# Fused Nystrom attention and SiLU layer: the first q and k loads on another queue, and the order of some early and later matmuls

## The chip, the cores and the metric

The kernel runs on one core of one Trainium2 chip. The metric is the device time of one execution in microseconds (us), lower is better. Every time below is in us unless it says ns.

## What is computed

```python
# q, k, v: (8 batches, 8 heads, 576 tokens, 64)
q_lm, k_lm = mean of q, k over groups of 18 tokens      # 32 landmarks
A  = softmax(scale * q    @ k_lm.T)                       # 576 x 32
Bm = softmax(scale * q_lm @ k_lm.T)                       # 32 x 32
C  = softmax(scale * q_lm @ k.T)                          # 32 x 576
Z  = Bm.T / (norm1(Bm) * norminf(Bm) + 1e-06)
for _ in range(6): Z = 2 * Z - Z @ Bm @ Z
x  = concat over heads of (A @ Z @ C @ v)                 # (4608, 512)
h  = x @ w_in                                             # (4608, 2048)
out = (h * sigmoid(h)) @ w_out                            # (4608, 512)
```

All inputs and the output are float32; the matmuls take bfloat16.

## The kernel before

**Order of work.** The kernel fixes the order of each engine's instructions by hand: an instruction stands on its engine where the Python code emits it. The loop has eight periods, one for each batch `b`. In period `b` the two big layers of batch `b` run (`l1_mm` makes `hps`, `l1_act` puts Silu of it into `gT`, `l2_mm` makes `ops`, which ScalarE copies to `ost` and SyncE stores), while the attention of batch `b + 1` (class `Att`) is worked out in between. A period has 16 steps `s`; `d` (2, 3, then 0) is the step at which the attention stages begin. `x @ w_in` is never formed directly: `m_unit` and `m_pair` make `mb`, a product of `zwT` with columns of `w_in`, and `l1_mm` multiplies it with `AT`, the transposed A.

**Counts.** After each step's `l1_mm` and `act`, `l2_mm(n)` emits up to `n` second-layer matmuls of 128x512 from a queue of finished token tiles; 16 of them make an output tile. How many each step emits stands in the lists `CNT` (periods 0 and 1) and `REST` (all others). These matmuls wait for nothing new, so they are what fills TensorE between dependent stages. In steps where ScalarE changes between Exp and Silu it loads a table (L151).

**The opening (L114 to L145, L759 to L845).** For batch 0 there is no earlier work to overlap. `load_qk(0)` issues four loads on POOL's DMA queue, in the order `j` = 1, 0, 3, 2: k and q of heads 0 to 3, then k and q of heads 4 to 7. Each is 128 rows (32 landmarks of four heads) of 18 tokens x 64, float32 in HBM and bfloat16 in the tile `nat`; the cast is done by the DMA. Behind them on POOL come `affine_select`, the load of v, the four quarters of w_in and the loads for batch 1. `idle` emits matmuls on a zero tile whose result is not used. For each part VectorE transposes `nat` into `qkT` (`transpose_qk`, L185) and TensorE sums 18 tokens with the identity into `lmp` (`landmarks_pe`); ScalarE scales the sum into `lmn` (`landmarks_out`, L202), VectorE transposes it into `lmc` (`lm_t`, L253). The lines L763 to L785 give VectorE's order: transpose of part 1, of part 0, `lm_t(0)`, transposes of parts 3 and 2, `lm_t(1)`. Then come `b_scores`, `c_scores`, the softmaxes and the iteration for Z (`ns_mm`, `ns_step`).

**Period 0, step 4 (`s == d + 2`, L955 to L988).** TensorE gets `a_shift(2)`, four second-layer matmuls, `f_mm`, `m_unit(2)`, `m_unit(3)` and `l1(4)`. Both units write the same two PSUM banks, so the second waits until VectorE and ScalarE have cast the first (L669). ScalarE then loads the Silu table.

**Step 3 of periods 2 to 6 (`s == d + 3`, L1036 to L1048).** `l1`, two Silu, two second-layer matmuls, `f_mm`, `b_scale`, `f_out`, the rest of the step's count (8 of 10), `ns_mm`. The next step starts with `l1(4)`, which needs the PSUM buffer that the first of the two Silu reads.

**Buffers.** The tags `lma` (POOL's landmark sums, L210) and `xs` (shifted scores of A, from batch 3 on, L529) are SBUF buffers of one copy each.

Of the kernel before, what the change touches and what calls it, by code (L numbers as in the profile page):

```python
# [8 lines left out]
FP = mybir.dt.float32  # L9
# [31 lines left out]
def kernel(  # L41
# [47 lines left out]
    def psn1(nm):  # L89
        return psn.tile([128, 512], FP, tag="n", name=nm)  # L90
# [7 lines left out]
    def load_qk(b, js=(1, 0, 3, 2)):  # L98
        if b not in nat_t:
            nat_t[b] = loadp.tile([128, 4, SEG * Dh], BF, tag="nat", name="nat")  # L100
        nat = nat_t[b]
        for j in js:
            src = (q, k)[j % 2]
            g = j // 2
            nc.gpsimd.dma_start(
                out=nat[:, j, :],
                in_=src[b, 4 * g:4 * g + 4].rearrange("h (l t) d -> (h l) (t d)", t=SEG))
# [3 lines left out]
        nc.gpsimd.dma_start(out=vt, in_=v[b].rearrange("h (p c) d -> p h (c d)", c=VC))  # L111
        v_t[b] = vt

    load_qk(0)  # L114

    zero = outp.tile([128, DM], FP, tag="ost", name="zero", bufs=3).bitcast(BF)[:, 0:512]
    nc.vector.memset(zero, 0.0)
# [63 lines left out]
    def transpose_qk(b, j):  # L181
        if b not in qkT_t:
            qkT_t[b] = loadp.tile([128, 4, S, 2], BF, tag="qkT", name="qkT")
        o = qkT_t[b][:, j, :, :].rearrange("p s e -> p (s e)").bitcast(FP)
        nc.vector.transpose(out=o.rearrange("p (l t) -> p t l", t=SEG),  # L185
                            in_=nat_t[b][:, j, :].bitcast(FP).rearrange("p (t l) -> p t l", l=L))
# [544 lines left out]
    def l2_mm(n):  # L731

        st = l2_state
        while n > 0 and st["queue"]:
# [16 lines left out]
                nc.sync.dma_start(out=out[r0:r0 + 128, :], in_=ost)  # L751


    CNT = {0: [0, 0, 0, 0, 4, 4, 2, 2, 4, 4, 2, 2, 2, 2, 2, 2],
           1: [2, 2, 2, 2, 2, 6, 8, 8] + [4, 3] * 4}
    REST = [5, 4, 12, 10, 3, 3, 3, 3, 4, 4, 4, 3, 4, 3, 4, 3]


    ORD = (1, 0, 3, 2)  # L759
    wt = pso1("idle")  # L760
    idle(wt, 12, 512)
    lp = psn1("lmp")
    transpose_qk(0, 1)  # L763
    landmarks_pe(0, lp, 0, 2)
    transpose_qk(0, 0)
    landmarks_out(0, lp, 0, 2)
    idle(wt, 3, 512)
    a = Att(0)
    a.lm_t(0)
    a.bd_expand(0, 1, nc.scalar.copy)  # L770
# [79 lines left out]
    for b in range(B):  # L850
# [14 lines left out]
        for s in range(NDC):  # L865
# [34 lines left out]
            elif not nxt or s == d:  # L900
                l1(s)
                act(s)
                l2_mm(cnt[s])
                if nxt and a.sub:
                    i = 1 if a.early else 0
                    if i == 0:
                        a.a_first()
                    a.a_scores(i)
                    a.a_max(i)
                    a.a_sub(i)  # L910

            elif s == d + 1:
                l1(s)
                act(s)
                l2_mm(cnt[s])
                if a.sub and not a.early:
                    a.a_scores(1)
                    a.a_max(1)
                    a.a_sub(1)
                if b == 0:  # L920

                    transpose_qk(1, ORD[s])
                    a.lm_t(1)
                    a.bd_expand(0, 2, nc.gpsimd.tensor_copy)
                    for i in (1, 2):
                        a0.a_scores(i)
                        a0.a_max(i)
                a.b_scores()
                a.c_scores()
                if a.early:  # L930
                    a.a_scores(2)
                a.b_max()
                a.c_max(0)
                table(AF.Exp)
                if b == 0:
                    for i in (1, 2):
                        a0.a_shift(i)
                        a0.a_exp(i)
                a.b_exp()
            elif s == d + 2 and a.sub:  # L940
                a.a_start()
                a.c_max(1)
                if not a.early:
                    l2_mm(4)
                    a.a_scores(2)
                a.a_max(2)
                a.a_sub(2)
                a.c_exp(0)
                a.c_exp(1)
                a.a_exp_all()  # L950
                a.b_norm()
                l2_mm(cnt[s] if a.early else cnt[s] - 4)
                table(AF.Silu)
                l1(s)
            elif s == d + 2:  # L955
                n = cnt[s]
                a.a_start()
                a.a_scores(0)
                a.a_scores(1)
                a.c_max(1)  # L960
                a.a_max(0)
                a.a_max(1)
                a.c_exp(0)
                a.c_exp(1)
                if b:
                    l2_mm(min(n - 4, 6))
                a.a_scores(2)
                a.a_max(2)
                a.a_shift(0)
                a.a_exp(0)  # L970
                l2_mm(2 if b else 0)
                a.a_shift(1)
                a.a_exp(1)
                a.b_norm()
                l2_mm(2 if b else 0)
                a.a_shift(2)
                a.a_exp(2)
                if b == 0:
                    a.b_scale()
                    l2_mm(n)  # L980
                    a.f_mm()
                    a.f_out()
                    a0.m_unit(2, nc.vector.tensor_copy, nc.scalar.copy)
                    a0.m_unit(3, nc.vector.tensor_copy, nc.vector.tensor_copy)
                else:
                    l2_mm(n - 4 - min(n - 4, 6))
                table(AF.Silu)
                l1(s)  # L988
            elif b == 0:
                l1(s)  # L990
                r = s - d
                if r == 3:
                    act(s - 1)
                    a.ns_mm()
                    a.c_transpose(0)
                    a.ns_step()
                    a.c_out(0, nc.scalar.copy)
                    a0.a_norm(1)
                    a0.a_norm(2)
                elif r == 4:  # L1000
                    a.ns_mm()
                    a.c_transpose(1)
                    a.w_scale()
                    a.ns_step()
                    a.ns_mm()
                    a.c_out(1)
                    a.a_norm(0)
                    a0.a_transpose(1)
                    a0.a_out(nc.scalar.copy)
                elif r == 5:  # L1010
                    a.ns_step()
                    a.ns_mm()
                    a.a_norm(1)
                elif r == 6:
                    a.w_mm()
                    a.ns_step()
                    a.ns_mm()
                    a.w_out()
                    a.ns_step()
                    a.a_norm(2)  # L1020
                elif r == 7:
                    a.ns_mm(last=True)
                    a.x_out()
                    a.a_transpose(0)
                    a.a_out(nc.scalar.copy)
                elif r == 8:
                    a.z_mm(psa1("zt"))
                    a.z_out()
                    l2_mm(cnt[s])
                    a.a_transpose(1)  # L1030
                    a.a_out(nc.vector.tensor_copy)
                act(s)
                if r in (9, 11):
                    a.m_pair(r - 9)
                l2_mm(cnt[s] if r != 8 else 0)
            elif s == d + 3:  # L1036
                l1(s)
                act(s - 1)
                act(s)
                l2_mm(2)  # L1040
                a.f_mm()
                a.b_scale()
                a.f_out()


                nc.gpsimd.tensor_copy(out=gate, in_=a.fx[:, :, 0])  # L1046
                l2_mm(cnt[s] - 2)
                a.ns_mm()  # L1048
            elif s <= d + 8:
                l1(s)  # L1050
                if s == d + 6:
                    a.w_mm()
                a.ns_step()
                act(s)
                if s == d + 4:
                    a.a_sum(0)
                elif s == d + 5:
                    a.a_sum(1)
                elif s == d + 6:
                    a.w_scale()  # L1060
                    a.w_out()
                    a.a_rec(0, 2)
                    a.a_mul(0)
                    a.a_mul(1)
                elif s == d + 7:
                    a.a_norm(2)
                l2_mm(cnt[s])
                a.ns_mm(last=(s == d + 8))
            elif s == d + 9:
                l1(s)  # L1070
                a.x_out()
                act(s)
                l2_mm(cnt[s])
            elif s == d + 10:
                l1(s)
                a.z_mm()
                a.z_out()
                act(s)
                l2_mm(cnt[s])
            else:  # L1080
                l1(s)
                act(s)
                if s in (d + 11, d + 13):
                    a.m_pair(s - d - 11)
                l2_mm(cnt[s])
# [67 lines left out]
```

## Time and profile before

| what | value |
|---|---|
| time, median of 3 runs | 269.35 us (268.81 to 271.1) |
| the profiled execution's own time | 269.39 us |
| its span (first to last instruction) | 267.4 us |
| TensorE busy | 250.0 us, 93% of the span |
| ScalarE, VectorE, POOL busy | 173.4, 161.6, 118.0 us |
| first-layer matmuls `hps` | 512, 286 ns mean |
| second-layer matmuls `ops` | 540, 379 ns mean |
| POOL's DMA queue, SyncE's DMA queue | 18.35 MB, 13.57 MB |
| granted TensorE clock, mean | 0.999 |

How to read the lines that follow. Times in a timeline count from the span's start: start, duration, engine, line, operation, tiles written and read, count, and in brackets the engine's idle time before it with what ended it. PE is TensorE, PEld its weight loads, DVE is VectorE, ACT is ScalarE, POOL is GpSimd, SP is SyncE. A matmul's duration contains its passage through the array, so matmuls that follow each other start closer together than they last. A waits line gives total wait, number of waits and the longest. A stretch gives, for each engine, busy time and number of instructions, then the granted clock, the DMA engines' mean busy share and the GB/s that they moved. DMA queue q0 is POOL's, q1 is SyncE's; a queue's line gives packets, MB and the packets' time as a share of 16 engines' time.

### The profile page before, as it was taken

The page shows a single profiled execution, that of the slowest core. Times are in us where ns is not written, and L with a number is a line of the kernel's source. Part 1 is how long each engine was busy: PE and PEld are TensorE (multiplying, and loading weights), DVE is VectorE, ACT ScalarE, POOL GpSimd, SP SyncE. Part 2 cuts the span into 40 slices and gives each one's busy share as a digit, 9 for nine tenths or more (in the row PEclk, how much of TensorE's full clock was granted, in tenths as well). Part 3 has the DMA queues.
Part 4 walks back from the last instruction along what each step waited for, and adds up shares of the span by engine and source line. Part 5 has one row for each costly group of instructions (what it writes and reads, how often), then busy time and mean ns, then how long its engine had stood idle before and what let it go on. Part 6 is the DMA issues. An engine that isn't in the chain of part 4 may idle for free.

```text
span 267.4 us, 6703 instructions
## 1 busy us (share of the span) xinstructions
PE 250.0 (93%) x2718; PEld 143.4 (54%) x2758; DVE 161.6 (60%) x395; ACT 173.4 (65%) x317; POOL 118.0 (44%) x169
## 2 busy tenths in 40 slices
PE   6788979999999989999999999999999999999994
PEld 2546645475555455455655565555555564555541
DVE  4677984548597867776786778686778654000000
ACT  2367966769657784869575956687577857646511
POOL 8517426114798079644874189408950030100000
PEclk9999999999999999999999999999999999999999
DMA  6999999974994954779197929313471612121122
GB/s 100 196 209 208 206 207 213 206 149 83 207 133 85 204 97 82 132 151 174 50 127 163 189 75 122 92 32 110 63 152 39 102 59 66 39 78 42 39 78 78
DMA packets 37790, 32.34 MB, mean 121 GB/s; under 512 B 18816, under 2 KB 29056, under 8 KB 37760
## 3 DMA queue, kind: packets, MB, share of 16 engines
q0 software_dynamic: 15104, 18.35, 42.5%
q1 hardware_dynamic: 22656, 13.57, 22.4%
q8 instruction: 21, 0.34, 0.5%
q14 instruction: 9, 0.07, 0.1%
HBM read 36.70 MB, written 9.44 MB: 173 GB/s over the span
## 4 chain that ended last, share of the span: by engine, by line
PE 77%; ACT 7%; DVE 6%; issue 4%; DMA 3%; POOL 1%; POOLq 0%; ACTq 0%; DVEq 0%
PE ops L77 39%; PE hps L77 23%; DMA nat<-in_q_dram 3%; ACT L151 3%; PE bb L77 3%; PE sa L77 3%; PE mp L77 2%; PE lmp L77 2%; DVE cmx L427 2%; PE wp L77 1%; PE scp L77 1%; ACT gT L723 1%; PE mpp L77 1%; DVE nm L570 1%; ACT ost L749 1%
## 5 line engine op out<-in xcount | busy, mean ns | idle before, releaser
L77 PE MATMUL ops<-w_out_sb,gT 128*128 128x512 bf16 x540 | 138.9, 379 | 3.3 <-issue 2.2
L723 ACT ACTIVATE gT<-hps 128x576 bf16<-128x576 f32 (+2 forms) x128 | 82.6, 651 | 58.1 <-PE hps L77 57.1
L77 PE MATMUL hps<-AT,mb 128*128 128x288 bf16 (+2 forms) x512 | 82.7, 286 | 2.3 <-ACT gT L723 2.1
L77 PEld LDWEIGHTS <-gT 128*128 128x128 bf16 x576 | 53.0, 98 | 47.4 <-issue 5.7
L77 PEld LDWEIGHTS <-mb 128*128 128x128 bf16 x512 | 47.9, 98 | 27.1 <-issue 4.2
L185 DVE STREAM_TRANSPOSE qkT<-nat 128x576 f32<-128x576 f32 x32 | 39.1, 1242 | 2.3 <-DMA nat<-in_k_dram 1.3
L622 POOL TENSOR_TENSOR an<-ex,arec 128x512 bf16<-128x512 bf16 (+2 forms) x24 | 21.1, 902 | 22.0 <-DVE arec L612 19.5
L749 ACT COPY ost<-ops 128x512 f32<-128x512 f32 x36 | 21.0, 583 | 12.2 <-PE ops L77 12.0
L386 DVE SCALAR_TENSOR_TENSOR fx<-fx,bb 128x320 bf16<-128x320 bf16 (+1 forms) x39 | 17.1, 438 | 17.4 <-PE bb L77 16.9
L211 POOL TENSOR_TENSOR lma<-nat 128x1152 f32<-128x1152 bf16 x10 | 23.7, 2374 | 0.0
L689 DVE CAST mb<-mp 128x512 bf16<-128x512 f32 x28 | 18.0, 685 | 9.2 <-PE mp L77 9.1
L151 ACT ACT_TABLE_LOAD x16 | 20.5, 1283 | 1.1 <-PEq L1137 0.8
L1046 POOL CAST gate<-fx 128x2 f32<-128x2 bf16 x6 | 1.1, 185 | 45.5 <-DVE fx L356 45.5
L570 DVE TENSOR_REDUCE nm<-sa 128x16 bf16<-128x512 f32 (+2 forms) x22 | 13.2, 613 | 9.8 <-PE sa L77 9.7
L261 POOL COPY bd<-lmc 32x128 bf16<-32x128 bf16 (+1 forms) x32 | 8.9, 279 | 17.3 <-DVE lmc L253 11.3
L77 PEld LDWEIGHTS <-fx 32*32 32x32 bf16 (+1 forms) x168 | 8.4, 93 | 12.0 <-DVE fx L386 2.0
L690 ACT CAST mb<-mpp 128x1024 bf16<-128x1024 f32 x14 | 14.2, 1011 | 0.6 <-PE mpp L77 0.6
L607 DVE TENSOR_REDUCE arec<-ex 128x16 f32<-128x512 bf16 (+2 forms) x24 | 14.1, 587 | 0.1
L77 PE MATMUL bb<-fx 32*32 32x64 bf16 (+2 forms) x168 | 13.1, 205 | 1.1 <-DVE fx L386 0.9
L77 PEld LDWEIGHTS <-qkT 128*128 128x128 bf16 (+1 forms) x160 | 10.0, 98 | 6.4 <-DVE xs L583 2.7
L77 PE MATMUL sa<-bd,qkT 128*128 128x128 bf16 (+1 forms) x152 | 12.3, 220 | 0.2 <-DVE xs L583 0.2
L427 DVE TENSOR_REDUCE cmx<-scp 128x1 f32<-128x576 f32 x16 | 11.9, 753 | 0.8 <-PE scp L77 0.5
(110 smaller groups left out, 254.9 us busy)
## 6 DMA issues: line engine op xcount, KB each, us to landing
out_dram<-ost SPq DMA_DIRECT2D x36, 256.0 KB, 2.4
nat<-in_k_dram POOLq DMA_DIRECT2D x16, 288.0 KB, 6.3
nat<-in_q_dram POOLq DMA_DIRECT2D x16, 288.0 KB, 7.9
v<-in_v_dram POOLq DMA_DIRECT2D x8, 576.0 KB, 7.4
w_in_sb<-in_moe_w_in_dram POOLq DMA_DIRECT2D x4, 512.0 KB, 15.1
w_out_sb<-in_moe_w_out_dram POOLq DMA_DIRECT2D x4, 512.0 KB, 13.5
AT<-an SPq DMA_TRANSPOSE x30, 4.3
eCT<-eC SPq DMA_TRANSPOSE x12, 4.1
```

The costliest lines, as they stand in the source:

```text
L77: nc.tensor.matmul(out=o, lhsT=lhsT, rhs=rhs, start=start, stop=stop, skip_group_check=True)
L151: nc.scalar.activation(out=spare[:, 1:2], in_=spare[:, 0:1], func=func)
L185: nc.vector.transpose(out=o.rearrange("p (l t) -> p t l", t=SEG), in_=nat_t[b][:, j, :].bitcast(FP).rearrange("p (t l) -> p t l", l=L))
L211: nc.gpsimd.tensor_tensor(out=a1, in0=nat[:, :, 0:3 * w], in1=nat[:, :, 3 * w:6 * w], op=OP.add)
L386: nc.vector.scalar_tensor_tensor(out=n, in0=self.fx, scalar=2.0, in1=self.p, op0=OP.mult, op1=OP.add if self.tiled else OP.subtract)
L427: nc.vector.tensor_reduce(out=mx, in_=self.s[g][:, :, 0:HF], op=OP.max, axis=AX.XY, negate=True)
L570: eng.tensor_reduce(out=self.nm[0:pr, c:c + n, :], in_=self.sa[i][0:pr, 0:256 * n].rearrange("p (c h l) -> p c h l", h=8, l=L), op=OP.max, ...
L622: nc.gpsimd.tensor_tensor(out=self.an[0:pr, c:c + n, :].rearrange("p c (h l) -> p (c h) l", l=L), in0=x, in1=r.unsqueeze(2).to_broadcast(( ...
L689: nc.vector.tensor_copy(out=o[:, r, 0:512], in_=m[r])
L690: nc.scalar.copy(out=o[:, :, 512:1024], in_=m2)
L723: nc.scalar.activation(out=gT_t[b][:, 2 * s:2 * s + 2, o + c0:o + c1], in_=h[:, :, 0:c1 - c0], func=AF.Silu)
L749: nc.scalar.copy(out=ost, in_=st["ps"])
```

## The change

1. k and q of heads 0 to 3 of batch 0 (parts 1 and 0) are loaded as float32 by SyncE's queue, into two borrowed buffers of 128 x 1152 float32 (tags `lma` and `xs`). VectorE casts k into `nat` and ScalarE casts q. POOL's queue keeps parts 3 and 2. One idle matmul less stands behind the first landmarks.
2. In period 0, step 4, `m_unit(2)` goes ahead of `f_mm`, two second-layer matmuls come behind `f_out`, and `m_unit(3)` goes behind `l1(4)`. Step 4 has 6 second-layer matmuls instead of 4, and step 9 has 2 instead of 4.
3. Period 2 gets a list of its own with 14 instead of 10 in step 3 and one less in steps 7, 9, 10 and 14. From period 3 on, step 3 has 12 instead of 10, and steps 6 and 7 one less each. The totals of each period stay.

```diff
-    load_qk(0)
+    nat_t[0] = loadp.tile([128, 4, SEG * Dh], BF, tag="nat", name="nat")
+    raw = [nsp.tile([128, 2, 9 * Dh], FP, tag="lma", name="raw", bufs=1)
+           .rearrange("p a n -> p (a n)"),
+           attp.tile([128, len(TCH), 256], FP, tag="xs", name="raw", bufs=1)
+           .rearrange("p c n -> p (c n)")[:, 0:SEG * Dh]]
+    for j in (1, 0):
+        nc.sync.dma_start(
+            out=raw[j], in_=(q, k)[j][0, 0:4].rearrange("h (l t) d -> (h l) (t d)", t=SEG))
+    load_qk(0, (3, 2))
...
-    CNT = {0: [0, 0, 0, 0, 4, 4, 2, 2, 4, 4, 2, 2, 2, 2, 2, 2],
-           1: [2, 2, 2, 2, 2, 6, 8, 8] + [4, 3] * 4}
-    REST = [5, 4, 12, 10, 3, 3, 3, 3, 4, 4, 4, 3, 4, 3, 4, 3]
+    CNT = {0: [0, 0, 0, 0, 6, 4, 2, 2, 4, 2, 2, 2, 2, 2, 2, 2],
+           1: [2, 2, 2, 2, 2, 6, 8, 8] + [4, 3] * 4,
+           2: [5, 4, 12, 14, 3, 3, 3, 2, 4, 3, 3, 3, 4, 3, 3, 3]}
+    REST = [5, 4, 12, 12, 3, 3, 2, 2, 4, 4, 4, 3, 4, 3, 4, 3]
...
     lp = psn1("lmp")
+    nc.vector.tensor_copy(out=nat_t[0][:, 1, :], in_=raw[1])
+    nc.scalar.copy(out=nat_t[0][:, 0, :], in_=raw[0])
     transpose_qk(0, 1)
     landmarks_pe(0, lp, 0, 2)
     transpose_qk(0, 0)
     landmarks_out(0, lp, 0, 2)
-    idle(wt, 3, 512)
+    idle(wt, 2, 512)
...
                 if b == 0:
                     a.b_scale()
-                    l2_mm(n)
+                    l2_mm(4)
+                    a0.m_unit(2, nc.vector.tensor_copy, nc.scalar.copy)
                     a.f_mm()
                     a.f_out()
-                    a0.m_unit(2, nc.vector.tensor_copy, nc.scalar.copy)
-                    a0.m_unit(3, nc.vector.tensor_copy, nc.vector.tensor_copy)
+                    l2_mm(n - 4)
                 else:
                     l2_mm(n - 4 - min(n - 4, 6))
                 table(AF.Silu)
                 l1(s)
+                if b == 0:
+                    a0.m_unit(3, nc.vector.tensor_copy, nc.vector.tensor_copy)
```

## The prediction

> **What bounds the kernel now.** I read the page first (busy shares, chain by line), then the timeline of the first 13 us, then TensorE's waits, then the DMA queues in short windows. The page and TensorE's waits from 85 us on:
>
> ```profile
> PE 250.0 (93%) x2718; PEld 143.4 (54%) x2758; DVE 161.6 (60%) x395; ACT 173.4 (65%) x317; POOL 118.0 (44%) x169
> ...
> PE 77%; ACT 7%; DVE 6%; issue 4%; DMA 3%; POOL 1%; POOLq 0%; ACTq 0%; DVEq 0%
> ```
> ```profile
> PE hps L77 <- ACT gT L723: 2.1, 5, 0.7
> ```
>
> TensorE sets the end: 93% busy, 77% of the chain. So an edit pays in two places only: in the opening, where nothing is ready for TensorE, and in the few gaps later. The five gaps of 2.1 us are one per period (0.71 at 96.36, 0.27 at 125.10, 153.83 and 182.56, 0.55 at 211.57): the first-layer product of step 4 waits for Silu of step 3, behind a table load. The opening, VectorE:
>
> ```profile
> 5.54 1.26 DVE L185 STREAM_TRANSPOSE qkT<-nat 128x576 f32<-128x576 f32 x1 [1.07 <-DMA nat<-in_k_dram]
> 7.04 1.26 DVE L185 STREAM_TRANSPOSE qkT<-nat 128x576 f32<-128x576 f32 x1 [0.24 <-DMA nat<-in_q_dram]
> 8.72 0.25 DVE L253 STREAM_TRANSPOSE lmc<-lmn 128x64 f32<-128x64 f32 x1 [0.43 <-ACT lmn L202]
> 9.24 1.26 DVE L185 STREAM_TRANSPOSE qkT<-nat 128x576 f32<-128x576 f32 x1 [0.27 <-DMA nat<-in_k_dram]
> 11.03 1.25 DVE L185 STREAM_TRANSPOSE qkT<-nat 128x576 f32<-128x576 f32 x1 [0.53 <-DMA nat<-in_q_dram]
> 12.13 0.21 DVE L253 STREAM_TRANSPOSE lmc<-lmn 128x64 f32<-128x64 f32 x1
> ```
>
> The four parts land one behind the other (k0, q0, k1, q1 below; 0 and 1 are the head groups), and VectorE takes them in that order. The landmark transpose at 12.13 releases b_scores and all that follows to the first Silu, so whatever moves 12.13 moves the end.
>
> **Part A, the loads.** Each part is 128 rows, 8 to each of 16 DMA engines. The stretches:
>
> ```profile
> 2.50:3.00 0.50, 0.50 (x3) 0.21 (x2) 0.21 (x3) 0.00 (x0) 0.50 (x2) 1.00 0.65 55
> 3.00:4.00 1.00, 1.00 (x4) 0.40 (x3) 0.00 (x0) 0.00 (x0) 0.93 (x4) 1.00 0.90 157
> ...
> 5.00:6.00 1.00, 0.35 (x2) 0.00 (x0) 0.47 (x1) 0.00 (x0) 1.00 (x2) 1.00 1.02 187
> ```
>
> The last two columns are the DMA share and GB/s written. From 4 us the engines are full, so POOL's issues (0.55 each) limit nothing: bandwidth does. 288 KB at 187 GB/s is 1.58 us, 0.2 for each row of an engine. A float32 row reads the same 4.6 KB, so I keep 0.2.
>
> When does SyncE's data start? SyncE is released at 0.8 (its only early wait is 0.8 long). The last store is issued at 264.3; DMA is at nothing in 264.5 to 265.0 and at 0.62 in 265.0 to 265.5, so 0.8 passes. Data from 1.6, against about 2.75 for POOL (issue 1.32). Until 2.75 an engine moves 5 of its 16 float32 rows at full pace; first rows are slower (55 GB/s above), I take 4. Then POOL's queue joins with k1, q1. How two queues share is shown at 47.5 to 48.3, a store under loads:
>
> ```profile
> DMA packets 96, 0.18 MB, mean 229 GB/s; under 512 B 12, under 2 KB 12, under 8 KB 96
> ...
> q0 software_dynamic: 48, 0.10, 77.1%
> q1 hardware_dynamic: 48, 0.09, 31.1%
> ```
>
> 48 packets each: one for one. So 12 rows left cost 12 x 0.4 = 4.8 and end at 7.55. For stragglers and the semaphore I add 0.85 (q0 now lands 1.1 after 2.75 + 16 x 0.2 = 5.95): **q0 lands at 8.4, not 7.04**. k0 lands near 5.2; its VectorE cast (0.6 to 1.3: 512 elements from PSUM take 0.685 at L689, 128 take 0.23 at L176) and transpose end by 7.8 at the latest, hidden under q0's wait. q0's ScalarE cast is on the path: 1152 elements between 1.01 (1024, L690) and 1.27 (1280, L591), so 1.15. Behind it in VectorE's order stand q0's transpose, the landmark transpose, k1's and q1's transposes and the one at 12.13. From q0's transpose to that one it is 12.13 - 7.04 = 5.09 now, less the DMA waits 0.27 and 0.53, since k1 and q1 then have landed: 4.3. Sum: 8.4 + 1.15 + 4.3 = 13.85, **1.7 us later**. q1 (landing about 9.5) is no longer what is late.
>
> Bounds: SyncE served wholly first, q0 lands 1.6 + 3.2 + 1.1 = 5.9, total 11.35, a gain of 0.8. All four parts ending together, 1.6 + 32 x 0.2 + 1.2 = 9.2, a loss of 2.5. I stay near the upper end because the 48 to 48 row is the nearest.
>
> The skill words sharing otherwise: by the Trainium skill, "DMA: Bandwidth & Descriptors" (Queues, rings and completion order), an engine drains a packet of about 9 to 17 descriptors before it switches. By it each part's 8 rows would go as a block and the sum would be that of rival 2; the 48 to 48 window speaks for single rows.
>
> At nothing: the dropped idle matmul (0.27 a piece at 8.15) stands on TensorE ahead of k1's landmarks, while VectorE's two transposes (2.3) run. SyncE's two issues have no store behind them until 45.2. POOL issues two loads fewer, so v and w_in are issued 1 us sooner; no engine waits for either now, and if they came late it would be w_mm and the w_in units. The borrowed buffers are first reused after 60 us.
>
> **Part B, period 0, step 4.** Now:
>
> ```profile
> 34.07 0.22 PE L77 MATMUL bb<-bmt 32*32 32x32 bf16 x8 [0.32 <-ACT ex L596]
> ...
> 35.43 0.41 PE L77 MATMUL mp<-w_in_sb,zwT 64*32 64x512 bf16 x8 [0.81 <-DVE mb L669]
> ...
> 37.24 0.49 PE L452 MATMUL ctp<-ident,eC 128*96 128x128 bf16 x6 [0.26 <-DVE mb L669]
> ```
>
> Gaps of 1.39. After: unit 2 fills the 0.32, and two second-layer matmuls (0.43 in the chain) and l1 stand ahead of unit 3, so the 0.81 goes. But VectorE's two casts of unit 3 (1.29) still come ahead of the transpose at 37.24, which I move by 0.2 only. TensorE then has done 0.43 more work 0.2 sooner: 0.63, of which step 9 (4 to 2 matmuls) gives the 0.43 back as time, unless ScalarE's copies there bind. I take 0.5; ends 0 and 0.65.
>
> **Part C, step 3 of periods 2 to 6.** Four more matmuls (0.86) in period 2 cover the 0.71; two (0.43) cover each 0.27, and 0.43 of 0.55: 0.71 + 3 x 0.27 + 0.43 = 1.95. Totals per period are unchanged, and the slots that give them up still hold l1 (0.49), ns_mm (0.14) and two matmuls (0.43), 1.06 against ScalarE's 0.65 and VectorE's 0.49 + 0.30 + latency. I leave 0.25 for small gaps: 1.7. Ends 1.0 and 1.95.
>
> Sum: +1.7 - 0.5 - 1.7 = -0.5 us. Against the profiled execution's 269.39 (span 267.4 and 2.0 around it; 0.04 above the median 269.35): **268.9 us**.
>
> **Rivals.**
> 1. *SyncE first*: the float32 rows win the engines, q0 lands at 5.9, A gains 0.8: 269.39 - 0.8 - 0.5 - 1.7 = 266.4. For it: SyncE starts 1.1 earlier; against it, the 48 to 48 row. Chance 0.20.
> 2. *Blocks of 8 rows*: the queues take turns by whole parts. At 2.75 four rows of k0 are left (0.8), then k1's eight (1.6), then q0's (1.6): 6.75, landed 7.6, A costs 0.9: 268.1. Against it the 48 to 48 row, though a store's rows are 2 KB, not 4.6. Chance 0.13.
> 3. *TensorE slows down in a longer gap* (slower). TensorE now stands still for 1.80 before the first landmarks, and idle matmuls behind it still take 0.27. With q0 at 9.55 cast it stands still from 5.34 for 4.2. At the start the idle matmuls' weight loads come 0.43 apart until 3.80, then four in 0.75: it begins slow and needs some 2.9 us of work. If the gap brings the slow pace back, the 18 landmark matmuls of 128 columns are 0.107 apart instead of 0.054 (a quarter of 0.43 and of 0.215), 0.95 more, and the two later groups, partly under VectorE's transposes, 0.15 more: A 2.8, 270.0. It decides where the gap passes some length between 1.8 and 4.2. Chance 0.15.
> The rule for it is in the Trainium skill, "TensorE: Matmul & The Clock Gate" (Part 1: The HAM clock gate): about 3.4 us without work halve the clock. No row here shows it for a later gap; the granted clock stays 1.00 throughout, even over the slow start.
> 4. *The gap only moves*: the slots left with two matmuls wait in turn, C yields 0.2: 270.4. For it, every ScalarE act waits for TensorE already (93 times), so nothing is spare on TensorE's side; against it, the 1.06 to 0.65 above. Chance 0.10.
>
> **How the numbers follow.** The forecast has 0.42 (its own range 268.0 to 269.7). 8 in 10 needs the rivals on both sides: 266.4 to 270.4. Over 1% (2.7 us, about what a measurement of this kernel can tell from no change) means under 266.7 or over 272.1. Under it lie most of rival 1 and the best ends of A, B and C together: 0.18. Over it only the worst ends, 2.5 in A with the slow pace and nothing from C: 0.04. Within: 0.78.
>
> **What would show it.** A: ScalarE's cast starts near 8.4, q0's transpose near 9.55, the landmark transpose now at 12.13 comes near 13.8; rival 1 has it by 11.5. Packets of both queues alternate from 2.8 on. Rival 3: landmark matmuls at 0.1 apart, not 0.05. B: no wait of 0.8 for the mb cast near 36. C: hps no longer waits for gT in step 4 of periods 2 to 6; rival 4 has new waits at steps 6 to 9. I am wrong if q0 lands before 7, or if part C's waits stay.

## The result

| kernel | median us | ratio to before, 95% interval |
|---|---|---|
| before | 269.40 (15 runs) | 1 |
| changed | 266.84 (15 runs) | 0.9906 (0.9881 to 0.9930) |

The change makes the kernel 0.94% faster, about 2.5 us. The forecast was 268.9, range 266.4 to 270.4: inside the range, with a gain five times as large as the forecast 0.5.

The profiled execution of the changed kernel took 265.98 (span 264.0). Its page, busy shares and chain by engine:

```profile
PE 254.0 (96%) x2757; PEld 143.1 (54%) x2757; DVE 161.5 (61%) x396; ACT 174.3 (66%) x318; POOL 117.0 (44%) x167
...
PE 86%; DVE 7%; ACT 2%; DMA 2%; issue 1%; POOL 0%; SPq 0%; ACTq 0%; POOLq 0%; DVEq 0%
```

TensorE now carries 86% of the chain instead of 77%, in a shorter span. (The profile before holds records of 540 of the 576 second-layer matmuls, this one of all 576. So the two busy sums are not to be compared, and part of the step from 77% to 86% can come of that.) Its waits from 85 us on:

```profile
PE hps L77 <- ACT eC L447: 0.2, 1, 0.2
PE sa L77 <- DVE xs L593: 0.2, 1, 0.2
```

All five waits of `hps` for `gT` are gone. The opening, VectorE:

```profile
4.89 0.81 DVE L774 CAST nat<-raw 128x1152 bf16<-128x1152 f32 x1 [1.48 <-DMA raw<-in_k_dram]
5.73 1.26 DVE L195 STREAM_TRANSPOSE qkT<-nat 128x576 f32<-128x576 f32 x1
7.46 1.26 DVE L195 STREAM_TRANSPOSE qkT<-nat 128x576 f32<-128x576 f32 x1 [0.47 <-ACT nat L775]
9.05 0.24 DVE L263 STREAM_TRANSPOSE lmc<-lmn 128x64 f32<-128x64 f32 x1 [0.34 <-ACT lmn L212]
9.22 2.30 DVE L195 STREAM_TRANSPOSE qkT<-nat 128x576 f32<-128x576 f32 x2
11.61 0.25 DVE L263 STREAM_TRANSPOSE lmc<-lmn 128x64 f32<-128x64 f32 x1
```

The landmark transpose stands at 11.61, not at the forecast 13.85. q0 landed at 6.25, its ScalarE cast ran from 6.28 for 1.15. The reason is in the DMA queues between 3 and 5 us, and between 5 and 6:

```profile
DMA packets 181, 0.76 MB, mean 380 GB/s; under 512 B 16, under 2 KB 16, under 8 KB 181
## 3 DMA queue, kind: packets, MB, share of 16 engines
q1 hardware_dynamic: 181, 0.76, 100.4%
```
```profile
q0 software_dynamic: 68, 0.16, 83.3%
q1 hardware_dynamic: 38, 0.10, 26.4%
```

From 3 to 5 us there is no packet of POOL's queue at all, although it had issued k1 at 1.33. Nearly all of SyncE's 16 rows an engine went through alone: POOL's first row came at 5.08, and 38 packets of SyncE's queue were left for 5 to 6. Period 0, step 4:

```profile
33.69 0.22 PE L77 MATMUL bb<-bmt 32*32 32x32 bf16 x8
33.84 0.60 PE L77 MATMUL ops<-w_out_sb,gT 128*128 128x512 bf16 x2
...
36.92 0.49 PE L462 MATMUL ctp<-ident,eC 128*96 128x128 bf16 x6 [0.70 <-DVE mb L679]
```

The wait of 0.81 before unit 3 is gone and one of 0.70 stands before the transposes. Against the profile before, the first `hps` of step 0 comes 0.45 sooner, of step 10 0.55, of period 1 0.55, and of period 7 (225.60 here) 3.28. So by the two profiles 0.5 us come from the opening, almost nothing from step 4, and the rest from periods 2 to 6. Two profiles are two executions, though, and the experiments correct the first of these.

### The profile page after: what moved, and what is told of

Its sections match the earlier page's. It is cut to its first block, busy times and chain, and to the rows that moved or that the text cites. A ratio compares the mean times of both kernels' runs of the same rounds, so it can differ in the third digit from the quotient of the medians.

```text
span 264.0 us, 6743 instructions
## 1 busy us (share of the span) xinstructions
PE 254.0 (96%) x2757; PEld 143.1 (54%) x2757; DVE 161.5 (61%) x396; ACT 174.3 (66%) x318; POOL 117.0 (44%) x167
## 4 chain that ended last, share of the span: by engine, by line
PE 86%; DVE 7%; ACT 2%; DMA 2%; issue 1%; POOL 0%; SPq 0%; ACTq 0%; POOLq 0%; DVEq 0%
PE ops L77 46%; PE hps L77 23%; PE bb L77 3%; PE sa L77 3%; PE lmp L77 3%; PE mp L77 2%; DVE cmx L437 2%; DMA raw<-in_q_dram 2%; DVE nm L580 2%; PE wp L77 2%; PE scp L77 1%; PE mpp L77 1%; PE atp L654 1%; DVE mb L679 1%; DVE xs L593 1%
## 5 line engine op out<-in xcount | busy, mean ns | idle before, releaser
L77 PE MATMUL ops<-w_out_sb,gT 128*128 128x512 bf16 x576 | 146.2, 380 | 0.1
```

The costliest lines, as they stand in the source:

```text
L77: nc.tensor.matmul(out=o, lhsT=lhsT, rhs=rhs, start=start, stop=stop, skip_group_check=True)
```

## The experiments

**1. One part at a time.** Four kernels take the change apart: A (loads), B (step 4 and the counts of period 0) and C (the counts of the other periods).

```diff
 loads_alone:   before + raw loads by SyncE, casts, idle(wt, 2, 512)
 counts_alone:  before + CNT[2] = [5, 4, 12, 14, ...], REST = [5, 4, 12, 12, 3, 3, 2, 2, ...]
 step4_alone:   before + m_unit(2), f_mm, l2_mm(n - 4), l1, m_unit(3); CNT[0] with 6 and 2
 loads_undone:  the changed kernel with load_qk(0) and idle(wt, 3, 512) as before
```

Expected of loads alone:

> Only part A of the change (k and q of heads 0 to 3 by SyncE's queue, cast on chip, one idle matmul less); steps and counts as before. Theory S (SyncE's rows are served before POOL's, as the changed kernel's packets show): q lands near 6.3, the landmark transpose at 12.13 comes near 11.6, 0.5 us faster than before, 268.9. Theory P (the prediction: both queues share row by row): q lands near 8.4, 1.7 us slower, 271.1.

Measured 269.22, ratio 1.0011 (0.9989 to 1.0032). Neither: no 1.7 lost and no gain that can be told. The rows were served as theory S says, and the landmark transpose stood at 11.65. What was wrong in S is the place it was measured from. In the four later profiles of kernels that load as before, the same transpose stood at 11.76 (counts alone), 11.44 (step 4 alone), 11.62 (loads undone) and 11.79 (experiment 4); in the four with part A and 12 idle matmuls at the start it was at 11.61 to 11.67. The 12.13 of the profile before was the latest of five.

Expected of the counts alone:

> Only part C (period 2's own list, REST with 12 in step 3). Theory T (the five gaps are worth their shown length plus about 0.16, the part of a matmul's shown duration that the next one could have overlapped): 0.86 + 3 x 0.43 + 0.43 to 0.70, 2.6 to 2.85 us faster, 266.7. Theory P (the gaps are worth their shown length, less 0.25 given back): 1.7 us faster, 267.7.

Measured 266.50, ratio 0.9899 (0.9872 to 0.9925), 2.7 us: theory T. The whole gain of the change is here. The same stretch of a period, from the timeline of the counts alone:

```profile
121.79 2.10 PE L77 MATMUL ops<-w_out_sb,gT 128*128 128x512 bf16 x9
123.73 0.30 PE L77 MATMUL bb<-fx 128*128 128x160 bf16 x2
123.87 0.65 PE L77 MATMUL hps<-AT,mb 128*128 128x288 bf16 x4
```

The `hps` starts at 123.87, 0.16 before the `bb` pair's shown end at 124.03. The profile before has this:

```profile
124.53 0.30 PE L77 MATMUL bb<-fx 128*128 128x160 bf16 x2
125.10 0.41 PE L77 MATMUL hps<-AT,mb 128*128 128x288 bf16 x2 [0.27 <-ACT gT L723]
```

There the pair ended at 124.83 and `hps` came at 125.10: a shown gap of 0.27, but TensorE could have taken a matmul from 124.67, so 0.43. Two matmuls at 0.215 fill just that. Read off at the first `hps` of each period, the lead over the profile before grows by 0.87 in period 2 and by 0.42 or 0.43 in each of periods 3 to 6, 2.58 in all. The last gap, shown as 0.55, gave no more than its two matmuls; 0.11 of it stays, which is too short for the list of waits.

Expected of step 4 alone, and of the changed kernel without its loads:

> Only part B (unit 2 ahead of f_mm, unit 3 behind l1, 6 and 2 matmuls in steps 4 and 9 of period 0). Theory V (VectorE's two casts of unit 3 set when the transposes after them start, so the step gives back what it gains): 0 to 0.2 us faster, 269.3, with a wait of 0.6 to 0.8 before the transposes. Theory P: 0.5 us faster, 268.9.

> The changed kernel with part A undone, B and C left in. If the parts add up (theories S, T, V): 0.5 us slower than the changed kernel, 2.8 us faster than before, 266.6. If part A's gain in the trace of the changed kernel is lost again further on (the opening is not what sets the end): as fast as the changed kernel within 0.2 us.

Measured 270.44, ratio 1.0042 (1.0023 to 1.0061): **slower** by 1.1 us, which neither theory had. And 267.84, ratio 0.9945 (0.9925 to 0.9964), 1.5 us faster, not 2.8: B costs about 1.2 on top of C. TensorE's waits from 30 to 48 us with step 4 alone, and the place of the longest:

```profile
PE ops L77 <- DMA w_out_sb<-in_moe_w_out_dram: 1.9, 2, 1.1
PE ctp L452 <- DVE mb L669: 0.7, 1, 0.7
```
```profile
33.45 0.22 PE L77 MATMUL bb<-bmt 32*32 32x32 bf16 x8
34.81 0.59 PE L77 MATMUL ops<-w_out_sb,gT 128*128 128x512 bf16 x2 [1.15 <-DMA w_out_sb<-in_moe_w_out_dram]
```

The fifth and sixth second-layer matmuls of step 4 need the second quarter of w_out. It landed at 34.77 here (34.61 before, where these two matmuls come only at 37.58). In the changed kernel it landed at 33.39, ahead of them. That quarter's sooner landing is what part A is worth to B: it landed at 33.4 to 34.3 in the five profiles with part A, and at 34.6 to 35.4 in the four with all of the loads as before. The likely reason is that POOL's queue carries two loads less, and that SyncE's first row comes at 1.84 against POOL's 2.77.

**2. Who is served first.** Three kernels change what the two queues hold, and a fourth moves four matmuls in the third; all start from the changed kernel.

```diff
 four_by_sync:
-    for j in (1, 0): nc.sync.dma_start(out=raw[j], ...)
-    load_qk(0, (3, 2))
+    for j in (1, 0, 3, 2): nc.sync.dma_start(out=raw[j], ...)   # casts: k by VectorE, q by ScalarE
 late_sync:
+    nc.vector.memset(raw[j][:, 0:1], 0.0)                       # behind ident2; the two loads wait for it
 only_k_by_sync:
-    nc.sync.dma_start of q;  nc.scalar.copy(out=nat_t[0][:, 0, :], in_=raw[0]);  load_qk(0, (3, 2))
+    load_qk(0, (0, 3, 2))
```

> All four parts of q and k of batch 0 go by SyncE's queue as float32 and are cast by VectorE (k) and ScalarE (q); POOL's queue then begins with v, issued at about 1.3. Theory E (a queue that has the engines keeps them until it is empty): no row of POOL's before about 7.5, when SyncE's 32 rows an engine are read, and v lands after 11. Theory D (POOL's queue has a start of its own that takes until about 5): rows of v from 5 on, between SyncE's. Theory P (row by row from 2.75): rows of v from 2.75 on. Time: two more casts (0.8 and 1.15) stand ahead of the transposes, so 0 to 1 us slower than the changed kernel by E.

Measured 269.32, ratio 0.9997 (0.9976 to 1.0017), so 2.4 us slower than the changed kernel by the ratios. q1 landed at 10.25 (9.11 in the changed kernel) and its cast stood behind that. A second cost is the clock: behind two standstills of TensorE, 0.92 until 10.29 and 1.06 until 12.47, the granted clock was 0.73, 0.50 and 0.91 in the stretches of 2 us from 12 to 18. The four executions with a mean granted clock of 0.997 or more took 268.2 to 268.5, the six with 0.993 or 0.994 took 269.1 to 270.1. The queues from 3 to 5.9 us, then from 7 to 8.5:

```profile
DMA packets 263, 1.08 MB, mean 372 GB/s; under 512 B 29, under 2 KB 29, under 8 KB 263
## 3 DMA queue, kind: packets, MB, share of 16 engines
q1 hardware_dynamic: 263, 1.08, 99.6%
```
```profile
q1 hardware_dynamic: 101, 0.44, 76.2%
q0 software_dynamic: 102, 0.08, 33.4%
```

None of the three theories holds throughout: SyncE's queue ran alone until about 6.1, though v had been issued at 1.67, and then the two moved equal numbers of packets, 101 to 102.

> SyncE's two loads wait for a one-column memset behind VectorE's constants, so they are issued near 3.5 instead of 0.8, when POOL's queue is already running (from about 2.75). Theory E1 (whoever came first is served first): no row of SyncE's until POOL's queue runs dry, far behind 6. Theory E2 (SyncE's queue always goes first): SyncE's rows alone from about 4.4 to 7.5, and POOL's stand still. Theory P (row by row, as a store did at 47.5 to 48.3): both queues' packets in equal number from 4.4 on. The time is worse than the changed kernel's in all of them, by 1 to 4 us, since q lands later.

Measured 274.66, ratio 1.0247 (1.0189 to 1.0305): about 9 us slower than the changed kernel by the ratios, and not the 1 to 4 expected, a miss. TensorE stood still for 7.96 before the first landmarks, and the granted clock was 0.75 from 8 to 10, 0.50 from 10 to 18 and 0.69 from 18 to 20, which is 5.1 us of full clock less. SyncE's loads were issued at 3.44 and 3.90. From 4.3 to 6.5, then from 7.5 to 9.5:

```profile
DMA packets 213, 0.41 MB, mean 184 GB/s; under 512 B 25, under 2 KB 43, under 8 KB 213
## 3 DMA queue, kind: packets, MB, share of 16 engines
q0 software_dynamic: 213, 0.41, 109.0%
```
```profile
q1 hardware_dynamic: 122, 0.51, 70.4%
q0 software_dynamic: 129, 0.10, 36.6%
```

Now POOL's queue, which was first, ran alone through k1 and q1, and sharing in about equal numbers began against v. So SyncE's queue has no precedence (against E2). In all three kernels the queue that started first kept the engines for its first 15 to 20 rows an engine, and sharing began after that. Turns in blocks (as in rival 2, but of about 16 rows) are not excluded: counts over 16 engines do not tell whether single rows or blocks alternate. What sets this length, and why the store's first packet came 1.4 after its issue at 45.16, in the midst of loads, was not tried and stays open.

> Only k of heads 0 to 3 goes by SyncE's queue (8 rows an engine); POOL's queue has q, k, q. Theory E: POOL's first row comes when SyncE's are through, near 3.6, q lands near 6 and needs no cast, its transpose starts at 7.0 behind k's instead of 7.46: 0.3 to 0.5 us faster than the changed kernel. Theory D: POOL's first row near 5, q lands near 7.2: as fast as the changed kernel within 0.3. Theory P: rows of both from 2.75, q lands near 6.2.

Measured 268.88, ratio 0.9997 (0.9970 to 1.0023): slower than the changed kernel by 2.4 us, a miss. POOL's rows began at 3.76, as E says, but at 104 packets in the two microseconds from 4 to 6 instead of 181 for SyncE's, and q0 landed at 8.28. Why they were slow there is open. Then a second cost joined. The stretches of this kernel (granted clock third from the right) and TensorE's timeline:

```profile
4.00:6.00 2.00, 2.00 (x6) 0.60 (x4) 1.63 (x2) 0.00 (x0) 2.00 (x4) 1.00 0.86 109
6.00:8.00 2.00, 0.17 (x1) 0.00 (x0) 0.39 (x1) 0.00 (x0) 1.24 (x2) 1.00 1.01 158
8.00:10.00 2.00, 1.59 (x19) 1.50 (x20) 1.26 (x1) 0.03 (x1) 0.56 (x2) 0.76 1.11 195
10.00:12.00 2.00, 2.00 (x22) 1.30 (x21) 1.66 (x3) 1.49 (x7) 1.09 (x2) 0.50 1.29 199
12.00:14.00 2.00, 2.00 (x47) 1.15 (x49) 1.05 (x2) 0.23 (x2) 0.39 (x3) 0.88 1.27 207
```
```profile
8.41 1.52 PE L77 MATMUL lmp<-nat,ident 128*128 128x128 bf16 x18 [2.24 <-DMA nat<-in_q_dram]
9.72 1.06 PE L77 MATMUL idle<-zero 128*128 128x512 bf16 x2
10.58 1.17 PE L77 MATMUL lmp<-nat,ident 128*128 128x64 bf16 x18
```

TensorE stood still for 2.24, and the clock was then granted at half. The means 0.76, 0.50 and 0.88 over 2 us each lack 0.48, 1.00 and 0.24 us of full clock, 1.72 in all; at half clock, each microsecond lacks 0.5, so the stretch was 3.4 us long. The landmark group that takes 0.69 in the changed kernel (9.07) takes 1.17. The stretch is not rare here: eight of the twelve executions had a mean granted clock under 0.995, and eleven of the next kernel's twelve.

> As the kernel with k alone by SyncE's queue, and in period 0, step 5, the four second-layer matmuls stand ahead of the transposes that wait for VectorE's casts of unit 3 (0.70 in the changed kernel) instead of behind them. Theory V: the wait is filled, 0.6 to 0.8 us faster than the kernel with k alone. Rival: ScalarE's copy of the transposes comes later by as much and the next steps wait for it: within 0.2 us.

```diff
                     a.ns_mm()
+                    l2_mm(cnt[s])
                     a.c_transpose(0)
                     a.ns_step()
...
-                l2_mm(cnt[s] if r != 8 else 0)
+                l2_mm(cnt[s] if r not in (3, 8) else 0)
```

Measured 268.77, ratio 0.9999 (0.9977 to 1.0020), against 0.9997 for the kernel that it is built on: the rival, within 0.2. The wait of 0.70 is filled, and two others take its place:

```profile
PE bb L77 <- DVE fx L392: 0.3, 1, 0.3
PE ctp L458 <- ACT eCT L463: 0.3, 1, 0.3
```

The first `hps` of step 6 came 0.75 sooner relative to step 5 than in the other, and step 7 had given it back: by these two waits, what bounds there is VectorE's sums (`fx`) and ScalarE's copy (`eCT`), not TensorE.

**3. Pairs.** What A and B are worth beside each other and beside C.

```diff
 loads_and_counts:     the changed kernel, step 4 and CNT[0] as before       (A, C)
 loads_and_step4:      the changed kernel, REST as before and no CNT[2]      (A, B)
 loads_counts_idle18:  (A, C) and idle(wt, 18, 512) instead of idle(wt, 12, 512)
```

> Parts A and C, step 4 of period 0 as before. Theory W (part A by itself does not move the end; it brings w_out forward, which part B alone needs; part C alone carries the gain): as part C alone, 2.4 to 2.8 us faster than before, 266.5, and no slower than the changed kernel. Rival: part A is worth about 1 us wherever the rest is tighter (as between the changed kernel and the one with its loads undone): 3.5 us faster, 265.5.

Measured 266.38, ratio 0.9901 (0.9885 to 0.9916): theory W. With C in place, A changes nothing (0.9899 without it), and the whole change (0.9906) is no better than C alone. In the profiles with part A the last of the five gaps is 0.28 shorter, with C and without; the times do not show it, and its reason was not sought.

> Parts A and B, counts of periods 2 to 7 as before. Theory W (part B costs 1.1 us because its second-layer matmuls wait for quarters of w_out, and part A lets those land 1.4 to 2 us sooner): no wait for w_out, 0 to 0.3 us from before, 269.2. Rival (the parts simply add up, +0.3 and +1.1): 270.5.

Measured 269.92, ratio 1.0029 (1.0012 to 1.0046): slower, between the two numbers. The waits for w_out fell from 1.9 to 0.4 as W says, but in this profile another transfer was late. Waits from 30 to 80 us:

```profile
PE wp L77 <- DMA eCT<-eC: 0.9, 2, 0.6
PE ctp L460 <- DVE mb L677: 0.7, 1, 0.7
...
PE ops L77 <- DMA w_out_sb<-in_moe_w_out_dram: 0.4, 1, 0.4
```

The two transposes by DMA of period 1 landed 9.1 after their issue, not 7.9 as before and in the changed kernel, among POOL's loads for batch 3. With A and C they took 8.3, and TensorE waited 0.3 for them. Whether that wait is there in most executions was not tried.

> Parts A and C, and 18 instead of 12 idle matmuls at the start, so that TensorE stands still for about 0.4 instead of 1.7 before the first landmarks. Theory G (in some executions a standstill of 1.7 to 2.2 in the opening brings a stretch of 3.4 us at half the clock, which costs 1 to 2 us): the highest times go, the median falls by 0.2 to 0.8 against parts A and C. Rival: no execution of parts A and C has such a stretch: the same within 0.2.

Measured 266.48, ratio 0.9910 (0.9889 to 0.9932): the rival, the same within 0.1 of A and C. The standstill of TensorE before the first landmarks went, and the first `hps` came at 23.57 instead of 23.07. These 0.5 did not reach the end in the two profiles (both spans are 264.6): A and C waited 0.3 for the transposes by DMA in period 1, and with 18 idle matmuls that wait is absent. Nor do the times bear out theory G. All five executions of A and C had a granted clock of 1.0, and one of the six with 18 idle matmuls had 0.994 (268.29).

**4. w_out sooner without part A.**

```diff
 step4_w_out_early (before, with part B):
-    load_w_in(3)                      # L782
+    load_w_out(0); load_w_out(1)
...
-    load_w_out(0); load_w_out(1)      # L821
+    load_w_in(3)
...
-    load_w_out(2); load_v(1); load_w_out(3)
+    load_w_out(2); load_w_out(3); load_v(1)
```

> Part B alone, and on POOL's queue the first two quarters of w_out ahead of the last quarter of w_in, and the last quarter of w_out ahead of v of batch 1; the loads of q and k as before. Theory W: both waits for w_out (1.15 and 0.80 with part B alone) go, 0.8 to 1.2 us faster than part B alone, within 0.3 of before, 269.1. Rival (part B is slow because of the order of unit 2 and unit 3, not because of w_out): 270.4.

Measured 270.28, ratio 1.0033 (1.0020 to 1.0046). Both waits for w_out went, but the time hardly followed, and not because of the order of the units: what was moved back was late in turn.

```profile
PE ctp L452 <- DVE mb L669: 0.7, 1, 0.7
PE wp L77 <- DMA v<-in_v_dram: 0.3, 1, 0.3
PE mp L77 <- DMA w_in_sb<-in_moe_w_in_dram: 0.3, 1, 0.3
```

These two waits are the difference to the changed kernel: from step 4 to step 10 of period 0, this kernel loses 0.33 more than the changed one between steps 4 and 5 (w_in) and 0.42 more between steps 8 and 9 (v), and elsewhere the same. Another part is the clock. Five of the twelve executions had a mean granted clock of 0.991 (270.3 to 270.7), the other seven a median of 269.91, and none of the 23 of before was under 0.997. The DMA engines are busy without a pause until 57 us, so another order of the loads moves the lateness instead of removing it. That part A helps because its first row comes 0.9 sooner is likely, not shown.

## Why the prediction was right or wrong

- **What bounds the kernel: right in the main.** TensorE sets the end and its gaps are what pays. That "whatever moves 12.13 moves the end" is too strong: with 18 idle matmuls the landmark transpose came at 12.14 instead of 11.64, and the span was the same.
- **A, +1.7: wrong.** The step that failed is "POOL's queue joins with k1, q1", row for row from 2.75 on. The 48 to 48 window of a store was the nearest row but not this situation, and not a rule even for that store: from 46.8 to 47.4 it had 57 packets to POOL's 33. In the changed kernel SyncE's rows went alone until 5, and q0 landed at 6.25 instead of 8.4. The terms behind it were sized well: ScalarE's cast 1.15 for 1.15, VectorE's 0.81 in 0.6 to 1.3, and 4.15 for 4.3 from q0's transpose to the landmark transpose. Rival 1 had q0 at 5.9. But its gain is not there either: A alone is 1.0011. The sum was made against 12.13, the latest of five executions of the same opening (11.44 to 12.13); against their mean, 11.75, the 11.64 of the four profiles with A and 12 idle matmuls is 0.1 sooner.
- **Costed at nothing: wrong in one place.** The prediction named v and w_in as what lands 1 us sooner, and no waiter. It left out w_out behind them in the same queue, and that part B moves two matmuls that read it ahead of its landing.
- **B, -0.5: wrong, in two steps.** The two matmuls were priced at 0.43 without asking whether their weights had landed; with B alone TensorE waited 1.9 for w_out, and B cost 1.1 us. And where the weights had landed, in the changed kernel, the transposes were to come 0.2 sooner. They came at 36.92 instead of 37.24, but 0.45 of that is the opening's: B made them 0.13 later, with a wait of 0.70. By the two profiles steps 4 to 10 gained 0.1 in all, and with A and C, B is worth nothing (0.9906 against 0.9901).
- **C, -1.7: right in place, mis-sized.** It measured 2.7. The term "0.71 + 3 x 0.27 + 0.43 = 1.95" took shown gaps. Four of the five are worth 0.16 more, the tail of the matmul before them, and the profiles give 2.58; only the last came out at its 0.43. The 0.25 set aside for new gaps was not needed, so rival 4 falls: the slots with two matmuls have no wait.
- **Rival 3: the mechanism is real, the trigger sooner.** It came not in the profiled execution of the changed kernel (standstill 1.69) but where q0 landed late (2.24, and 1.94 in the kernel with the matmuls first). Two of the changed kernel's 15 executions, with 267.92 and 269.02, had a mean granted clock of 0.994, the others 0.997 or more. The row for the rule of the Trainium skill, "TensorE: Matmul & The Clock Gate" (Part 1: The HAM clock gate), is the stretch above: its length, 3.4, agrees with the page's window of about 3.4 us. That it takes such a window of standing still does not agree: 2.24 was enough here.
- **Sum.** -0.5 was forecast and -2.5 measured: C gives 2.7, A and B together take 0.2 at most. The direction was right because C alone outweighs the rest. That the time lies inside the range is luck: the lower end, 266.4, was set by rival 1 with a gain in A, and A gains nothing that can be told; the time came there by the mis-sized C.

The version without part B and with A (266.38) or without both (266.50) is as fast as the changed kernel (266.84) within the intervals; none beats it beyond doubt.

## What to carry to other kernels

Price a gap on TensorE from the start of the last matmul and its pitch, not from its shown end: here 0.27 shown was 0.43 of work. Before a matmul is moved forward, look up when each thing it reads lands, weights too: the gap that it fills may lie just ahead of a transfer. And take the moment that a sum is made against from several profiles; the same opening varied by 0.7 us here, more than the effect that was sought.

## What the runs showed of the hardware that was not expected

- Two DMA queues do not always share from the first row on: the one that starts first had the engines alone for 15 to 20 rows of 4.6 KB an engine, then they moved equal numbers of packets (101 to 102). Equal shares are no rule: a store under loads had 57 packets to 33 before, and 104 to 29 in the changed kernel (46 to 47 us).
- Two loads of 576 KB of float32 by SyncE's queue moved 0.76 MB in 2 us (380 GB/s); POOL's casting loads read 374 GB/s (187 written, from 5 to 6 us before), so at these rates the conversion in the DMA costs next to nothing.
- A standstill of 2.24 us of TensorE was followed by 3.4 us at half the granted clock, and so was one of 1.94; 1.69 and 1.80 were not, in one profile each. Two shorter ones close together (0.92 and 1.06) were enough as well. The kernel before is not free of it: in one set of 29 executions, six had a mean granted clock of 0.991 to 0.994 and took 270.2 to 270.9, the others 268.3 to 269.4.
